# A stored order of steps in place of a list scheduler, in a fused attention and feed-forward kernel

## The chip, the cores and the metric

The kernel runs on one core of one Trainium2 chip. The metric is the device time of one execution in microseconds; the median of several runs is given, and one further execution was recorded by the hardware profiler. Engines are named as the profile names them: PE is TensorE (PEld its weight loads), DVE is VectorE, ACT is ScalarE, POOL is GpSimd, and SP is SyncE, which here only issues DMA transfers.

## What is computed

Attention with a soft cap on the scores, over 4 batches, 12 heads, 448 positions and 64 columns a head, then a feed-forward block with a sigmoid gate on the 1792 x 768 result:

```python
def _attn_ref(q, k, v, cap) -> np.ndarray:
    scale = 1.0 / np.sqrt(q.shape[-1])
    scores = scale * np.matmul(q, k.transpose(0, 1, 3, 2))
    scores = cap * np.tanh(scores / cap)
    scores = scores - np.max(scores, axis=-1, keepdims=True)
    attn = np.exp(scores)
    attn = attn / (np.sum(attn, axis=-1, keepdims=True) + 1e-09)
    return np.matmul(attn, v).astype(np.float32)

def _moe_ref(x, w_in, w_out) -> np.ndarray:   # x is attention's output, 1792 x 768
    h = x @ w_in                              # 768 x 2048
    g = h * (1.0 / (1.0 + np.exp(-1.702 * h)))
    return (g @ w_out).astype(np.float32)     # 2048 x 768
```

All inputs and the output are f32. The soft cap is 30, so the exponentials need no row maximum.

## The kernel before, in words

**Units.** The attention runs in 24 units, one for a batch and a pair of heads. The first 8 units multiply in f32; the other 16 split each operand into an f16 part and an f16 remainder and multiply the parts. For one unit, `scores` writes products of K and Q to PSUM (`s`, two banks in turn), ACT takes the tanh (`t`) and the exponential, and the result lies as `p`, in a ring of five tiles. In f16 units the exponential is split: a copy `p<-t` makes the high part (a step that ACT or DVE may do), and DVE's subtraction `p<-t,p` the low one. `row_sums`, `part_sums` and a few others multiply `p` by ones to get the row sums (`sm`), and `col_tiled` multiplies `p` by V (`pa`). The sums take a way through DRAM: `f<-sm`, then the transfers `sd`, `rsum`, a reciprocal `rr`, `rd`, and `rb`, the inverse sums spread over the partitions. DVE multiplies `pa` by `rb`, and the result is split again (`x` or `xa`, high and low).

**Feed-forward.** The weights arrive as raw words and are decoded on DVE and ACT (`g` and `wo` for the first pieces of `w_in`; `wi_h` and `wi_l` are the parts). For batches 0 and 1, `h_unit` multiplies x by `w_in` into `m`, the gate follows on ACT and DVE (`f`, `g`), and `o_unit` multiplies `g` by `w_out`, in `m` as well. Batches 2 and 3 share sums of blocks, seven products in place of eight, in `m` and `z`; they fill the time from about 400 us on.

**Shapes on the PE array.** Full products (`m`, `z`, most of the f16 `s`) use the whole 128 x 128 array. `pa` uses tiles of 128 rows by 64 columns, `sm` tiles of 128 by 32, and the f32 `s` tiles of 64 by 128 or 64 by 64. A step carries the shape's name in its field `turn`.

**What sets the order.** Nothing of this is issued as it is written. The class `Plan` records every step as an `Op`: the engines that may do it, with a cost on each (`ways`), its dependences, and the rings of buffers from which it takes tiles. `scaled` (L194) records a step with two ways, ACT (`on_act`) and DVE (`on_dve`), unless it is told one. `mm`, `act`, `dve` and `dma` record steps for PE, ACT, DVE and SP. When all is recorded, `schedule` (L331) decides: 30 times a list scheduler (`forward`, L243) takes the step that can start first by the costs, with the engine among its ways and the ring slot that is free, and `backward` (L295) works out by when each step is due, which gives the priorities of the next pass. The best pass is kept. Then `refine` (L412) tries to move short runs of PE steps of one tile shape next to another run of that shape, up to 20 us away, and keeps a move if `timed` (L367) gives a shorter total. In these costs a change of tile shape on PE is put down at a fixed price:

```python
PE_TURN = 0.093
...
                if e == "PE":
                    us += PE_TURN * (o.turn != turn)
                    turn = o.turn
```

`emit` (L451) then issues the steps in that order, under a manual schedule, and each engine runs its own in a row. `keep_busy` can put small matmuls into gaps early on, and adds none in this kernel. A flag computed at the end guards a general path, which does not run with these inputs. In the profile nearly all instructions have the line of the helper that issues them: L218 for matmuls, L183 for DVE, L175 and L199 for ACT, L202 to L206 for `scaled` steps on DVE, L224 for transfers.

Of the kernel before, what the change touches and what calls it, by code (L numbers as in the profile page):

```python
# [35 lines left out]
PASSES = 30  # L36
# [21 lines left out]
DVE_SHY = (1.0,)  # L58
STAY = (0.0,)
ROUNDS, RUN, REACH = 4, 6, 20.0  # L60
# [48 lines left out]
class Plan:  # L109
# [118 lines left out]
    def start_over(self):  # L228
        bufs = {b for o in self.ops for b in o.bufs}
        for b in bufs:  # L230
            b.left, b.freed = 0, 0.0
            if b.ring:
                b.slot = None
        for o in self.ops:
            o.left, o.ready = len(o.deps), 0.0
            o.eng = next(iter(o.ways)) if len(o.ways) == 1 else None
            for b in o.bufs:
                b.left += 1
        for r in self.rings:
            r["free"] = [(0.0, i) for i in range(len(r["tiles"]))]  # L240
            r["queue"] = list(r["turns"])

    def forward(self, shy, stay=0.0):  # L243

        self.start_over()
        free = {"PE": 0.0, "ACT": ACT_FROM, "DVE": ACT_FROM, "SP": 0.0}
        cand = {e: [o for o in self.ops if e in o.ways and not o.left] for e in free}
        turn, pipe = None, 0.0
        order = []
        while len(order) < len(self.ops):  # L250
            best = None
            for e, c in cand.items():
                for o in c:
                    t = max(o.ready + (shy if e == "DVE" and len(o.ways) > 1 else 0.0), free[e])
                    for b in o.bufs:
                        if b.slot is None:
                            r = b.ring
                            t = max(t, r["free"][0][0]) if r["free"] and (r["any"] or r["queue"][0] is b) else math.inf
                    k = (t, o.prio + (stay if e == "PE" and o.turn != turn else 0.0), o.ways[e][0])
                    if best is None or k < best[0]:  # L260
                        best = (k, e, o)
            assert best is not None and best[0][0] < math.inf, "no step can go on"
            (t, _, us), e, o = best
            for w in o.ways:
                cand[w].remove(o)
            o.eng, o.emit = e, o.ways[e][1]
            for b in o.bufs:
                if b.slot is None:
                    b.ring["queue"].remove(b)
                    b.slot = b.ring["free"].pop(0)[1]  # L270
            if e == "PE":
                us += PE_TURN * (o.turn != turn)
                turn = o.turn
            o.start, o.end = t, t + us
            free[e] = t + us
            done = t + us + LAG[e]
            if e == "SP":
                pipe = max(pipe, t + us) + o.mb / DMA_BW
                done = pipe + LAG[e]
            order.append(o)  # L280
            for u in o.users:
                u.left -= 1
                u.ready = max(u.ready, t + us if u.eng == e == "PE" else done + HANDOFF)
                if not u.left:
                    for w in u.ways:
                        cand[w].append(u)
            for b in o.bufs:
                b.left -= 1
                b.freed = max(b.freed, done + HANDOFF)
                if not b.left and b.ring:  # L290
                    b.ring["free"].append((b.freed, b.slot))
                    b.ring["free"].sort()
        return order

    def backward(self, order):  # L295

        after = {o: [(u, 0.0 if u.eng == o.eng == "PE" else LAG[o.eng] + HANDOFF) for u in o.users] for o in order}
        turns = {}
        for o in order:
            for b in o.bufs:  # L300
                if b.ring:
                    x = turns.setdefault((id(b.ring), b.slot), [])
                    if not x or x[-1][0] is not b:
                        x.append((b, []))
                    x[-1][1].append(o)
        for x in turns.values():
            for (_, was), (_, then) in zip(x, x[1:]):
                for o in was:
                    after[o].append((then[0], LAG[o.eng] + HANDOFF))
        before = {o: [] for o in order}  # L310
        for o, xs in after.items():
            for u, lag in xs:
                before[u].append((o, lag))
        left = {o: len(xs) for o, xs in after.items()}
        end = max(o.end for o in order)
        due = {o: end for o in order}
        free = dict.fromkeys(("PE", "ACT", "DVE", "SP"), end)
        cand = [o for o in order if not left[o]]
        start = {}
        while cand:  # L320
            o = max(cand, key=lambda o: (min(due[o], free[o.eng]), o.end))
            cand.remove(o)
            free[o.eng] = start[o] = min(due[o], free[o.eng]) - (o.end - o.start)
            for q, lag in before[o]:
                due[q] = min(due[q], start[o] - lag)
                left[q] -= 1
                if not left[q]:
                    cand.append(q)
        return start

    def schedule(self):  # L331

        best = None
# [33 lines left out]
    def timed(self, pre, seqs, limit=math.inf):  # L367
# [5 lines left out]
        turn, pipe, left = None, 0.0, n  # L373
        while left:
            moved = False
            for e, s in seqs.items():
                k = at[e]
                while k < len(s):
                    i = s[k]
                    t = free[e]  # L380
                    for p, near in pre[i]:
                        if start[p] is None:
                            t = None
                            break
                        x = end[p] if near else done[p] + HANDOFF
                        if x > t:
                            t = x
                    if t is None:
                        break
                    o = self.order[i]  # L390
                    us = o.ways[e][0]
# [4 lines left out]
                    free[e] = t + us  # L396
                    if e == "SP":
                        pipe = max(pipe, t + us) + o.mb / DMA_BW
                        done[i] = pipe + LAG[e]
                    else:  # L400
                        done[i] = t + us + LAG[e]
                    if end[i] > limit:
                        return None
                    k += 1
                    left -= 1
                    moved = True
                at[e] = k
            if not moved:
                return None
        return start, end, max(end)  # L410

    def refine(self, rounds):  # L412

        pre = self.edges()
        seqs = {e: [i for i, o in enumerate(self.order) if o.eng == e] for e in ("PE", "ACT", "DVE", "SP")}
        start, end, best = self.timed(pre, seqs)
        for _ in range(rounds):
            gained = False
            k = 1
            while k < len(seqs["PE"]):  # L420
                s = seqs["PE"]
                turn = lambda j: self.order[s[j]].turn
                if turn(k) == turn(k - 1):
                    k += 1
                    continue
# [18 lines left out]
            if not gained:  # L444
                break
# [1110 lines left out]
```

## Time and profile before

| what | value |
|---|---|
| time, median of 3 runs | 603.84 us (603.43 to 603.88) |
| the profiled execution | 603.16 us, of which 600.9 us is the span from first to last instruction |
| PE busy | 589.3 us (98%) |
| DVE busy | 540.5 us (90%) |
| ACT busy | 414.2 us (69%) |
| TensorE's granted clock, mean | 0.998 |
| chain that ended last | PE 86%, DVE 5%, DMA 4% |

The 2.3 us between the span and the time lie outside of the recorded instructions. Busy shares are an average over the span: attention ends a little after 400 us, and the engines beside PE have more room behind that. Line numbers in rows are those of the kernel before.

### The profile page before, as it was taken

What the parts mean: (1) busy time and instruction counts of PE and PEld (TensorE: products, weight loads), DVE (VectorE), ACT (ScalarE), POOL (GpSimd) and SP (SyncE); (2) the same over time, 40 slices, a digit from 0 to 9 for tenths busy, and PEclk for the clock granted to TensorE, in tenths of its full rate; (3) what the DMA queues carried; (4) which work ended last, traced back from release to release, by engine and by line L of the source; (5) the groups of instructions that cost most, each with busy time, mean ns of one, the idle gap of its engine ahead of it and who ended that gap; (6) DMA issues with size and microseconds to landing.
All of it is one profiled execution on the core that took longest, in us unless ns stands there. A gap on an engine that the chain in (4) does not pass through costs nothing.

```text
span 600.9 us, 9852 instructions
## 1 busy us (share of the span) xinstructions
PE 589.3 (98%) x3666; PEld 281.5 (47%) x3666; DVE 540.5 (90%) x898; ACT 414.2 (69%) x610; POOL 0.2 (0%) x4
## 2 busy tenths in 40 slices
PE   7999999999999999999999999999999999999995
PEld 3332344444544444445554445455555555555552
DVE  4999999999999999999999989878999999968912
ACT  5998896999987987999879779834555554211100
POOL 0000000000000000000000000000000000000000
PEclk9999999999999999999999999999999999999999
DMA  8988864226567443513343453022222210001001
GB/s 297 383 234 246 296 220 149 81 53 208 154 193 231 157 130 87 178 46 109 109 122 130 127 174 120 30 83 58 71 76 65 53 54 1 31 15 47 32 15 50
DMA packets 45556, 73.87 MB, mean 123 GB/s; under 512 B 14952, under 2 KB 31168, under 8 KB 45504
## 3 DMA queue, kind: packets, MB, share of 16 engines
q1 hardware_dynamic: 45504, 73.20, 38.4%
q8 instruction: 30, 0.49, 0.3%
q14 instruction: 22, 0.18, 0.1%
HBM read 61.22 MB, written 11.95 MB: 122 GB/s over the span
## 4 chain that ended last, share of the span: by engine, by line
PE 86%; DVE 5%; DMA 4%; ACT 2%; issue 1%; SPq 1%; DVEq 0%; ACTq 0%
PE m L218 43%; PE z L218 22%; PE s L218 9%; PE pa L218 9%; PE sm L218 3%; DMA wo<-in_moe_w_in_dram 1%; DMA rd<-rr 1%; ACT t L175 1%; SPq L224 1%; DVE ta L183 1%; DMA stg<-in_kx_dram 1%; DVE p L183 1%; ACT p L175 1%; DMA wo<-in_q_dram 1%; DVE f L183 0%
## 5 line engine op out<-in xcount | busy, mean ns | idle before, releaser
L218 PE MATMUL m<-g,wo 128*128 128x448 f16 x624 | 127.4, 353 | 0.0
L218 PEld LDWEIGHTS <-wo 128*128 128x128 f16 x864 | 81.8, 98 | 82.0 <-issue 9.0
L175 ACT ACTIVATE t<-s,tsc 128x896 f32<-128x896 f32 x96 | 86.8, 918 | 17.4 <-PE s L218 13.7
L218 PEld LDWEIGHTS <-wi_h 128*128 128x128 f16 x528 | 49.4, 98 | 56.2 <-issue 12.2
L218 PE MATMUL m<-x,wi_h 128*128 128x448 f16 x234 | 63.6, 353 | 0.0
L175 ACT ACTIVATE t<-t,lnb,capt 128x896 f32<-128x896 f32 (+1 forms) x58 | 59.4, 1030 | 0.4
L183 DVE TENSOR_TENSOR p<-t,p 128x896 f16<-128x896 f32 (+1 forms) x58 | 55.2, 954 | 4.1 <-ACT p L199 3.7
L218 PE MATMUL m<-xa,wi_h 128*128 128x448 f16 x198 | 53.7, 353 | 0.0
L218 PE MATMUL s<-qh,kk 128*128 128x448 f16 (+3 forms) x160 | 48.1, 403 | 0.0
L199 ACT ACTIVATE p<-t 128x896 f16<-128x896 f32 (+1 forms) x54 | 45.1, 838 | 0.3
L183 DVE SCALAR_TENSOR_TENSOR wo<-wo 128x1024 int32<-128x1024 int32 (+2 forms) x42 | 43.8, 1064 | 0.0
L218 PE MATMUL m<-x,wi_l 128*128 128x448 f16 x117 | 41.2, 352 | 0.0
L218 PEld LDWEIGHTS <-stg 128*128 128x128 f16 x288 | 28.2, 98 | 26.3
L218 PE MATMUL s<-ql,kk 128*128 128x448 f16 (+1 forms) x128 | 39.6, 352 | 0.0
L218 PEld LDWEIGHTS <-wi_l 128*128 128x128 f16 x264 | 25.8, 98 | 24.1
L199 ACT ACTIVATE xa<-x 128x1024 f16<-128x1024 f32 x9 | 9.5, 1057 | 38.3 <-PE z L218 27.3
L218 PE MATMUL pa<-p,vh 128*64 128x448 f16 x256 | 35.6, 356 | 0.4 <-DVE rb L183 0.4
L218 PE MATMUL m<-xa,wi_l 128*128 128x448 f16 x99 | 34.9, 352 | 0.0
L218 PEld LDWEIGHTS <-kk 128*128 128x128 f16 (+1 forms) x256 | 20.8, 100 | 23.4 <-issue 6.8
L218 PE MATMUL sm<-p,ones 128*32 128x224 f16 (+2 forms) x544 | 30.8, 313 | 0.5 <-ACT p L175 0.5
L218 PEld LDWEIGHTS <-xa 128*128 128x128 f16 x216 | 21.1, 98 | 19.6
L175 ACT ACTIVATE p<-t,capt 128x896 f32<-128x896 f32 (+1 forms) x32 | 29.6, 970 | 0.0
(282 smaller groups left out, 1078.4 us busy)
## 6 DMA issues: line engine op xcount, KB each, us to landing
wo<-in_moe_w_in_dram SPq DMA_DIRECT2D x18, 512.0 KB
stg<-in_kx_dram SPq DMA_DIRECT2D x16, 448.0 KB
stg<-in_qx_dram SPq DMA_DIRECT2D x16, 448.0 KB
stg<-in_moe_w_out_dram SPq DMA_DIRECT2D x16, 384.0 KB
wo<-in_moe_w_out_dram SPq DMA_DIRECT2D x16, 384.0 KB
sum<-xa SPq DMA_DIRECT2D x32, 192.0 KB
stg<-sum SPq DMA_DIRECT2D x32, 192.0 KB
rb<-rd SPq DMA_DIRECT2D x44, 112.0 KB
```

Of the source, the lines that this page charges most:

```text
L175: self.nc.scalar.activation(real(out), real(in_), func, scale=real(scale), **b)
L183: getattr(self.nc.vector, name)(out=real(out), **{k: real(x) for k, x in ins.items()}, **kw, **a)
L199: self.nc.scalar.activation(real(out), real(in_), AF.Copy, scale=1.0 if f is None else f, **b)
L218: self.nc.tensor.matmul(real(o), real(w), real(x), start=a, stop=z)
L224: self.nc.sync.dma_start(real(o), real(i))
```

## The change

The list scheduler (`start_over`, `forward`, `backward`, `refine` and their constants) is taken out. In its place stands `ORDER`, a packed table with two parts: for each position, the number of a recorded step, its top bit saying which of the step's ways is taken; then, for each turn of each ring, the slot that it gets. `schedule` reads it, sets engine and slot of each step, lets `timed` work out start times along these rows, and sorts by them. The recording of the steps, their costs, their dependences and `emit` are as before. In the core of the diff one line of the table stands for all:

```diff
-PASSES = 30
...
-DVE_SHY = (1.0,)
-STAY = (0.0,)
-ROUNDS, RUN, REACH = 4, 6, 20.0
+
+ORDER = (
...
+    "ki+XIFzmw1TBXsd@Z^xe5gQD*3AaNRo_dCZ!(SO558+Jz2#bGrF#mV>AJ%H1p#"
+)
...
     def schedule(self):
 
-        best = None
-        for i in range(PASSES):
-            stay = STAY[i % len(STAY)] if i else 0.0
-            order = self.forward(DVE_SHY[0], stay)
-            total = max(o.end for o in order)
-            if best is None or total < best[0]:
-                best = (total, stay, {o: o.prio for o in order})
-            for o, t in self.backward(order).items():
-                o.prio = t
-        for o, p in best[2].items():
-            o.prio = p
-        self.order = self.forward(DVE_SHY[0], best[1])
-        self.refine(ROUNDS)
+        n = len(self.ops)
+        raw = zlib.decompress(base64.b85decode(ORDER))
+        slots = iter(raw[2 * n:])
+        for r in self.rings:
+            for b in r["turns"]:
+                b.slot = next(slots)
+        self.order = []
+        for x in struct.unpack(f"<{n}H", raw[:2 * n]):
+            o = self.ops[x & 0x7FFF]
+            o.eng = list(o.ways)[x >> 15]
+            o.emit = o.ways[o.eng][1]
+            self.order.append(o)
+        seqs = {e: [i for i, o in enumerate(self.order) if o.eng == e] for e in LAG}
+        start, end, self.total = self.timed(self.edges(), seqs)
+        for i, o in enumerate(self.order):
+            o.start, o.end = start[i], end[i]
+        self.order = [self.order[i] for i in sorted(range(n), key=lambda i: (start[i], i))]
```

The instructions themselves are the same, but for the 15 more `scaled` steps that go to DVE than before. What the table moves is shown at four places. A row is one instruction, or several alike that follow one another: its line, its operation, what it writes and reads, and the shape of what it writes; the number behind a name is that of the tensor.

**First, SP at the head of the program, before.** `wo` is a ring of staging tiles here, into which `k`, `q` and `v` of the f32 units are loaded; `g` takes the first four pieces of `w_in`.

```order
L524 DMA capt<-in_cap_dram 128x1
L224 DMA wo<-in_k_dram 128x448
L224 DMA wo<-in_q_dram 128x448
L224 DMA wo<-in_v_dram 128x512
L224 DMA wo<-in_k_dram 128x448
L224 DMA wo<-in_q_dram 128x448
L224 DMA g<-in_moe_w_in_dram 128x1024 x4
```

And SP at the head after:

```order
L408 DMA capt<-in_cap_dram 128x1
L263 DMA wo<-in_k_dram 128x448
L263 DMA wo<-in_q_dram 128x448
L263 DMA g<-in_moe_w_in_dram 128x1024 x2
L263 DMA wo<-in_v_dram 128x512
L263 DMA wo<-in_k_dram 128x448
L263 DMA wo<-in_q_dram 128x448
L263 DMA g<-in_moe_w_in_dram 128x1024 x2
```

Two of the four pieces of `w_in` have moved ahead of the first `v` and the second `k` and `q`.

**Second, PE in the f32 units, some 60 rows from its start, before.** Here `s`, `pa` and `sm` read K, V and ones.

```order
L218 MATMUL s_160<-wo 128x448 x2
L218 MATMUL pa_156<-p_136,wo 64x448 x2
L218 MATMUL sm_155<-p_137,ones_2_75 32x224 x4
L218 MATMUL sm_155<-p_138,ones_2_75 32x224 x4
L218 MATMUL s_161<-wo 128x448 x2
L218 MATMUL s_160<-wo 128x448 x2
L218 MATMUL sm_155<-p_134,ones_2_75 32x224 x4
L218 MATMUL sm_155<-p_135,ones_0_73 32x224 x2
L218 MATMUL sm_155<-p_135,ones_1_74 32x224 x2
L218 MATMUL pa_156<-p_137,wo 64x448 x2
L218 MATMUL pa_156<-p_138,wo 64x448 x2
```

PE at the same distance from its start, after:

```order
L257 MATMUL pa_156<-p_138,wo 64x448 x2
L257 MATMUL pa_156<-p_134,wo 64x448 x2
L257 MATMUL pa_156<-p_135,wo 64x448 x2
L257 MATMUL pa_156<-p_136,wo 64x448 x2
L257 MATMUL s_161<-wo 128x448 x2
L257 MATMUL s_160<-wo 128x448 x2
L257 MATMUL sm_155<-p_137,ones_2_75 32x224 x4
L257 MATMUL sm_155<-p_138,ones_2_75 32x224 x4
L257 MATMUL sm_155<-p_134,ones_2_75 32x224 x4
L257 MATMUL sm_155<-p_135,ones_0_73 32x224 x2
L257 MATMUL sm_155<-p_135,ones_1_74 32x224 x2
```

The eleven rows have six stretches of one shape before and three after.

**Third, PE in the f16 units, where the row sums of one `p` tile end, before.** Each f16 matmul has a weight load of its own ahead of it.

```order
L218 LDWEIGHTS ones_2_78
L218 MATMUL sm_155<-p_135,ones_2_78 32x224
L218 LDWEIGHTS wo
L218 MATMUL m_92<-g,wo 128x448
L218 LDWEIGHTS wo
```

And where the row sums of the last `p` tile of a unit end, after:

```order
L257 LDWEIGHTS ones_1_77
L257 MATMUL sm_155<-p_138,ones_1_77 32x224
L257 LDWEIGHTS vh_147
L257 MATMUL pa_156<-p_135,vh_147 64x448
L257 LDWEIGHTS vh_147
```

Before, the sums stop after `p_135`, twelve matmuls of `m` follow, and the sums of `p_136` come after them; after, the sums of all tiles stand together and `pa` follows them at once.

**Fourth, DVE in an f16 unit, before.** `ta` collects sums of `t`.

```order
L183 TENSOR_TENSOR p_138<-t_131,p_138 128x896
L183 SCALAR_TENSOR_TENSOR ql_130<-stg_123,qh_128 128x896
L183 TENSOR_TENSOR ta_133<-ta_133,t_132 64x448
L183 TENSOR_TENSOR p_134<-t_132,p_134 128x448
L183 TENSOR_TENSOR ta_133<-ta_133,t_132 64x448
```

The same tiles after:

```order
L222 TENSOR_TENSOR ta_133<-ta_133,t_132 64x448
L222 TENSOR_TENSOR p_138<-t_131,p_138 128x896
L243 CAST p_134<-t_132 128x448
L222 TENSOR_TENSOR ta_133<-ta_133,t_132 64x448
L222 TENSOR_TENSOR p_134<-t_132,p_134 128x448
```

The cast of `p_134` to its high part, on ACT before, has moved into DVE's row, two instructions ahead of the subtraction that reads it.

## Rows read from the trace of the kernel before

**Rows 1.** The page: busy time by engine, and the chain by engine.

```profile
PE 589.3 (98%) x3666; PEld 281.5 (47%) x3666; DVE 540.5 (90%) x898; ACT 414.2 (69%) x610; POOL 0.2 (0%) x4
...
PE 86%; DVE 5%; DMA 4%; ACT 2%; issue 1%; SPq 1%; DVEq 0%; ACTq 0%
```

**Rows 2.** PE's waits after its start: releaser, us in total, times, longest.

```profile
PE s L218 <- ACT t L175: 1.1, 2, 0.8
PE sm L218 <- ACT p L175: 0.5, 1, 0.5
PE pa L218 <- DVE rb L183: 0.4, 2, 0.2
```

**Rows 3.** Windows (from:to, length, busy by engine, PE's clock, DMA share, GB/s).

```profile
0.00:20.00 20.00, 16.37 (x100) 6.65 (x100) 10.84 (x37) 13.98 (x18) 0.20 (x4) 1.00 0.89 328
20.00:350.00 330.00, 328.22 (x2166) 150.72 (x2165) 323.56 (x514) 291.20 (x418) 0.00 (x0) 1.00 0.52 163
350.00:601.00 251.00, 244.72 (x1404) 124.17 (x1402) 206.08 (x350) 109.02 (x176) 0.00 (x0) 1.00 0.18 54
```

**Rows 4.** Pieces of the chain: start, duration, what (matmuls in a row).

```profile
16.81 1.71 PE s L218 x8
...
68.38 0.90 PE pa L218 x4
69.28 0.95 PE s L218 x4
...
75.16 0.89 PE sm L218 x16
...
77.86 1.65 PE pa L218 x8
...
110.51 1.65 PE sm L218 x32
...
126.83 1.26 PE pa L218 x12
...
148.52 0.30 PE sm L218 x8
...
162.81 0.50 PE sm L218 x16
...
170.29 1.14 PE m L218 x6
171.43 2.39 PE pa L218 x24
173.82 1.24 PE m L218 x6
```

**Rows 5.** DVE's groups by form: shapes, count, busy us, mean ns, idle before.

```profile
L206 DVE TENSOR_SCALAR wo<-wo 128x1024 f32<-128x1024 f32 x5 | 3.5, 691 | 0.0
L206 DVE TENSOR_SCALAR kk<-stg 128x896 f16<-128x896 f32 x5 | 3.1, 620 | 0.0
...
L204 DVE CAST p<-t 128x896 f16<-128x896 f32 x4 | 2.5, 618 | 0.0
...
L206 DVE TENSOR_SCALAR g<-f 128x448 f16<-128x448 f32 x5 | 1.9, 378 | 0.0
...
L202 DVE TENSOR_SCALAR f<-sm 128x224 f32<-128x224 f32 x2 | 0.8, 387 | 0.0
L206 DVE TENSOR_SCALAR wo<-stg 128x384 f16<-128x384 f32 x2 | 0.7, 356 | 0.0
```

**Rows 6.** Timeline of DVE's first decoding step: start, us, [idle before it].

```profile
9.23 0.43 DVE L183 TENSOR_SCALAR g<-g 128x512 int32<-128x512 int32 x1 [5.00 <-DMA g<-in_moe_w_in_dram]
```

**Rows 7.** Timeline at a `pa` that waits for DVE, from 292.0 us.

```profile
292.01 0.62 DVE L183 TENSOR_TENSOR rb<-pa,rb 128x448 f32<-128x448 f32 x1
...
292.54 1.08 DVE L183 TENSOR_TENSOR p<-t,p 128x896 f16<-128x896 f32 x1
...
292.68 0.57 PE L218 MATMUL pa<-p,vh 128*64 128x448 f16 x4 [0.16 <-DVE rb L183]
```

More of the change, by code (lines that the diff above doesn't have):

```diff
@@ L1 @@
+import base64
 import math
+import struct
+import zlib
 from contextlib import ExitStack
@@ L225, in dma @@
         self.op({"SP": (DMA_ISSUE * len(pairs), emit)}, [p[0] for p in pairs], [p[1] for p in pairs], mb=mb)
[L228 to L238, printed above, removed]
-        for r in self.rings:
-            r["free"] = [(0.0, i) for i in range(len(r["tiles"]))]
-            r["queue"] = list(r["turns"])
@@ L243, in forward @@
[L243 to L250, printed above, removed]
-            best = None
[L252 to L329, printed above, removed]
@@ L365, in edges, with timed @@
         return [list(dict(sorted(p)).items()) for p in pre]
-    def timed(self, pre, seqs, limit=math.inf):
+    def timed(self, pre, seqs):
         n = len(self.order)
@@ L372, in timed @@
         free = {"PE": 0.0, "ACT": ACT_FROM, "DVE": ACT_FROM, "SP": 0.0}
-        turn, pipe, left = None, 0.0, n
-        while left:
+        turn, pipe = None, 0.0
+        while any(at[e] < len(s) for e, s in seqs.items()):
             moved = False
             for e, s in seqs.items():
[L377 to L389, printed above, removed]
+                while at[e] < len(s) and all(start[p] is not None for p, _ in pre[s[at[e]]]):
+                    i = s[at[e]]
                     o = self.order[i]
+                    t = max([free[e]] + [end[p] if near else done[p] + HANDOFF for p, near in pre[i]])
                     us = o.ways[e][0]
@@ L395, in timed @@
                     start[i], end[i] = t, t + us
-                    free[e] = t + us
+                    free[e] = done[i] = t + us
                     if e == "SP":
[L398 to L405, printed above, removed]
+                        done[i] = pipe = max(pipe, t + us) + o.mb / DMA_BW
@@ L406, in timed @@
+                    done[i] += LAG[e]
+                    at[e] += 1
                     moved = True
-                at[e] = k
-            if not moved:
-                return None
+            assert moved, "no step can go on"
         return start, end, max(end)
[L412 to L425, printed above, removed]
-                m = k
-                while m < len(s) and turn(m) == turn(k):
-                    m += 1
-                run, tries = s[k:m], []
-                if len(run) <= RUN:
-                    for step in (-1, 1):
-                        j = k - 1 if step < 0 else m
-                        while 0 <= j < len(s) and abs(start[s[j]] - start[s[k]]) < REACH:
-                            if turn(j) == turn(k):
-                                tries.append(s[:j + 1] + run + s[j + 1:k] + s[m:] if step < 0 else s[:k] + s[m:j] + run + s[j:])
-                                break
-                            j += step
-                for new in tries:
-                    got = self.timed(pre, {**seqs, "PE": new}, best + 2.0)
-                    if got and got[2] < best - 0.005:
-                        (start, end, best), seqs["PE"], gained = got, new, True
-                        break
-                k = m
-            if not gained:
-                break
-        for i, o in enumerate(self.order):
-            o.start, o.end = start[i], end[i]
-        self.order = [self.order[i] for i in sorted(range(len(start)), key=lambda i: (start[i], i))]
-        self.total = best
```

39 lines of the change are left out of this document (37 added, 2 removed).

## Prediction, made before the changed kernel was run

> **What bounds the kernel now.** I read the page first: TensorE (PE) is busy for 589.3 of 600.9 us, VectorE (DVE) for 540.5, ScalarE (ACT) for 414.2, and 86% of the chain that ended last is PE [rows 1]. PE's busy time alone proves little, since a matmul's end is modelled and matmuls overlap, so I looked next at what PE waits for. After the first score matmuls there are three entries, 1.1, 0.5 and 0.4 us [rows 2]. PE runs one matmul after another, and its granted clock is 1.00 (the 2.4 GHz level) in every stretch [rows 3], so the clock is not in question. The time can fall in two ways: PE's stream gets cheaper, or its few waits go. The same windows show who comes second. From 20 to 350 us DVE is busy for 323.56 of 330.00 us [rows 3], so it has 6.4 us of room there. After 350 us it has 45 us, and before 20 us it mostly waits for its first weights: 5.00 us ahead of its first decoding step at 9.23 [rows 6].
>
> The chain of waits then shows a price inside PE's stream that no idle time shows. Six full-array products `m` that follow one another take 1.14 us, and the same six right after a row of `pa` (128x64 tiles) take 1.24 [rows 4]. A change of tile shape costs 0.10 us.
>
> **Part 1: fewer changes of tile shape.** The matmuls are the same 3401 in both kernels, and only their order differs. I counted along PE's order the places where the tile shape (rows x columns of the array) differs from that of the matmul before: 188 before, 104 after. The two places of PE in the section on the change show the pattern: `s`, `pa` and `sm` alternate before, and stand together now. By shape and type, runs before and after, with the price from the chain [rows 4]:
> - full array: 68 to 32. Price 1.24 - 1.14 = 0.10. 36 x 0.10 = 3.6 us.
> - 128x64 with f16 (`pa`): 33 to 17. Twelve cost 1.26 and 24 cost 2.39, so 12 cost 1.13 and the change 0.13. 16 x 0.13 = 2.1 us.
> - 128x32 with f16 (`sm`): 26 to 11. Eight cost 0.30 and 16 cost 0.50, so the change costs 0.10. 15 x 0.10 = 1.5 us.
> - 128x64 with f32: 21 to 11. Four cost 0.90 and eight 1.65, so the change costs 0.15. 10 x 0.15 = 1.5 us.
> - 128x32 with f32: 16 to 13. Sixteen cost 0.89 and 32 cost 1.65, so 0.13. 3 x 0.13 = 0.4 us.
> - the two f32 shapes of `s`: 25 to 23. Four cost 0.95 and eight 1.71, so 0.19. 2 x 0.19 = 0.4 us.
>
> The sum is 9.5 us; with the price of each kind averaged over all its runs in the trace it is 9.8, and I take **9.6 us**. It lies wholly on the path, since PE has no room to hide it. By place in the order, about 66 of the lost changes (7.8 us) lie before 350 us, the stretch in which DVE is nearly full, and 16 (1.8 us) between 350 and 400 us.
>
> **Part 2: fifteen scaling steps go from ACT to DVE.** DVE has 892 instructions for 877, ACT 594 for 609. By form: seven more casts of `p` at 128x896 (0.618 us), two at 128x448 (no row; the nearest, a scaling of that size, has 0.378), four more `f<-sm` (0.387), four more 128x448 scalings to f16 (0.378) and four more at 384 columns (0.356), 9.6 us in all [rows 5]. Against them stand two fewer 128x896 scalings (0.620), two of 1024 columns (0.691), one of 512 (between these and 0.378, taken as 0.42) and one `pu` copy (like the casts, 0.62): 3.7 us. The net is +5.9 us of durations. DVE's next instruction starts before the last one ends: `rb` runs from 292.01 to 292.63 and the next begins at 292.54 [rows 7]. With 0.08 of overlap for each of 15 steps, DVE's own time grows by **4.7 us**. ACT loses about 8 us, which is worth nothing by itself: it is busy for 291 of 330 us in the same stretch [rows 3].
>
> The Trainium skill, "VectorE: DVE Perf Modes", section "The DRAIN you can't avoid", says that the next DVE operation does not start until the pipe of the one before is empty, except where it isn't held. Taken as it stands for each added step it would make the 4.7 us the full 5.9, and the forecast below about 1 us longer; the rows at 292.54 go against it at that place.
>
> **Part 3: what DVE gives back.** A matmul that needs a DVE result comes at the later of two times: PE's own work ahead of it, and DVE's work up to and with that result plus DVE's idle time. For each such matmul I added PE's work ahead (rates and prices of [rows 4], from the first matmul at 5.15 us) and DVE's work (each step by its row of the same form, less the overlap), along the order of either kernel. The difference is the cushion. The smallest ones, before and after:
> - near 120 us: 127.1 - 120.6 = 6.5 before; 115.3 - 111.5 = 3.8 after
> - near 200 us: 202.4 - 195.8 = 6.6; 204.3 - 199.9 = 4.4
> - near 287 us: 287.6 - 280.3 = 7.3; 287.2 - 282.7 = 4.5
> - near 303 us: 303.4 - 295.7 = 7.7; 301.8 - 297.0 = 4.7
> - near 350 us: 13.3 before; 6.6 after. Later ones are 14.9 or more in both.
>
> The third of them can be laid against the trace: that `pa` starts at 292.68, 0.16 us after PE fell idle, right behind `rb`, which ends at 292.63 [rows 7]. So PE stood 5.1 us behind its own work there, and DVE 12.3 us. With the new order and DVE still 12.3 us behind, the awaited `rb` ends at 282.7 + 12.3 = 295.0, and PE, whose own work says 287.2, is 7.8 us behind: **2.7 us** more than before. The fourth gives 2.4 in the same way. Had DVE's steps kept their places in front of PE's needs, the cushion would have shrunk by the whole 7.8 + 4.7 us; it shrinks by 2.2 to 2.9 up to 305 us, so the new order brings what PE awaits earlier in DVE's row.
>
> At the head the first pieces of `w_in` (`g`) are issued after two loads in place of five, so DVE's 5.00 us of waiting [rows 6] shrinks; two pieces still come behind four others, and the head's decode steps now stand next to one another and wait for each other. I take 0.3 us, nearer to nothing than to the 2 us by which the first piece may come earlier. The given-back time is 2.7 - 0.3 = **2.4 us**, with bounds of 0 (all hidden) and 4.7 (every moved step paid).
>
> Past 440 us the smallest loop from PE through DVE back to PE tightens as well, by my count from about 7 us of slack to about 1; I price that at nothing, with 1.5 us as its upper bound. SP issues the same transfers in another order. Behind the head, the row sums' way through DRAM (`sd`, `rsum`, `rd`, `rb`) has 8.5 to 11.8 us of DVE work between the reciprocal and the product that needs `rb`, where it had 7 to 8.3, so it is priced at nothing; if `rb` came late, PE would stand at its `pa` as at 292.68 [rows 7]. The tail behind the last product is the same steps in both, at nothing too.
>
> **Sum.** The profiled run took 603.16 us. 603.16 - 9.6 + 2.4 = 595.96 us. That run lies 0.68 us under the median of the runs (603.84), so the forecast for the median is **596.6 us**, with 594.2 (nothing given back) to 598.9 (4.7 given back) as its own range.
>
> **Rivals.**
> - **A, nothing is given back.** DVE starts so much earlier at the head, or has so much slack in its idle 6.4 us, that PE keeps all 9.6: 594.2 us. For it: PE before waits for DVE only 0.4 us in all [rows 2]. Against it: the cushions at 290 to 305 us have no slack in the trace [rows 7].
> - **B, VectorE is the true bound from 20 to 350 us.** Then every result that PE awaits comes later by the 4.7 us added, less 0.3 at the head, what PE saves before 350 us is lost in waiting, and only the 1.8 us after it remain: 603.84 + 4.4 - 1.8 = 606.4 us, slower. For it: 323.56 of 330.00 us busy [rows 3]. Against it: the count above, by which DVE's order has moved ahead by most of the difference. It decides where the cushion shrinks by some 10 us rather than 2.7.
> - **C, the rows of one shape hold buffers.** `sm` and `pa` of a unit now stand together, so they need all five `p` buffers filled, and a split of `p` (1.08 us [rows 7]) may be exposed in each of the 16 f16 units: 17.3 - 9.6 gives 611.5 us; it breaks even at 0.6 us for each unit. Against it: `pa` already runs 24 in a row before [rows 4], with all five filled.
> - **D, gain and losses cancel:** half of B or C, near 603.8 us.
>
> **How the numbers follow.** Forecast 0.75, A 0.12, B 0.05, C 0.03, D 0.05. About 0.2% (1.2 us) is what a measurement of this kernel can tell from no change. The forecast and A lie beyond it on the fast side: faster 0.87, same 0.05, slower 0.08. The range goes from 593.5 (A with a little more from the head) to 601.5 (the forecast with the 4.7 us, the 1.5 us past 440 and the price of the overlap), which leaves out B, C, D and a little of the forecast's tail.
>
> **What the profile after would show.** Part 1 is right if `m x6` still costs 1.14 or 1.24, the long rows of one shape stand in the chain, and PE's busy time falls to near 580. Part 2: DVE near 545, ACT near 406. Part 3: PE's waits for DVE rise from 0.4 to 2 to 3 us, mostly on `pa`, `sm` and `m` between 80 and 310 us. If PE waits 5 us or more for DVE there, B has begun; if it waits for `p` from ACT or DVE at every unit's `sm`, C. The forecast is wrong if a change of shape costs less when `sm` and `pa` stand next to each other, or if DVE waits for ACT, DMA or PSUM where it did not before.

## The result

The kernel with the stored order took 595.57 us (median of 4 runs, 595.3 to 596.48), the kernel before 603.86 us in the same session (603.43 to 604.53). The ratio is 0.9864, with a 95% interval of 0.9847 to 0.9881: faster by 1.2 to 1.5%. The forecast for the median was 596.6. The execution that the profiler recorded took 595.59 us; the prediction's sum for it was 595.96.

The page of the changed kernel, busy time by engine and the chain that ended last by engine, to lay beside [rows 1]:

```profile
PE 580.4 (98%) x3666; PEld 288.4 (49%) x3666; DVE 545.3 (92%) x913; ACT 406.5 (69%) x595; POOL 0.2 (0%) x4
...
PE 72%; DVE 16%; DMA 6%; issue 3%; SPq 1%; ACT 1%; DVEq 0%
```

PE is busy for 8.9 us less, DVE for 4.8 more and ACT for 7.7 less, near the 580, 545 and 406 that the prediction named. (The rule of the Trainium skill, "VectorE: DVE Perf Modes", section "The DRAIN you can't avoid", taken for every added step without the exception that the page makes for steps that aren't held, would have made DVE's added time the full 5.9 us. The 4.8 sides with the overlap seen in [rows 7].) PE's share of the chain has fallen from 86% to 72%, so more of what released PE was somewhere else. What PE waits for after its start, to lay beside [rows 2] (engine, line, releaser: us in all, times, longest):

```profile
PE s L257 <- ACT t L214: 2.1, 3, 1.2
...
PE m L257 <- DVE f L222: 0.6, 2, 0.5
PE m L257 <- DVE x L222: 0.5, 1, 0.5
PE pa L257 <- DVE rb L222: 0.2, 1, 0.2
```

PE's waits for DVE are 1.3 us where they were 0.4, and its largest entry is `s` waiting for ACT. Two things are to be told apart, then: how cheap PE's stream became, and how much later it runs. For the second I use one measure throughout. **Lateness** is the start of a matmul less PE's own work ahead of it (every matmul and every change of shape at the prices of [rows 4], from 5.15 us on). It grows by what PE loses in waits, or to a lower clock, whatever a row calls them. In us, at marks of PE's own work:

| kernel | own work in all | at 20 | 40 | 60 | 98 | 200 | 287 | 350 | 575 |
|---|---|---|---|---|---|---|---|---|---|
| before | 589.4 | 2.0 | 3.1 | 4.2 | 4.2 | 4.3 | 4.8 | 5.1 | 5.3 |
| changed | 579.6 | 2.3 | 3.7 | 5.7 | 6.5 | 6.4 | 6.9 | 7.2 | 7.4 |

The profiled executions differ by 7.57 us. Own work accounts for 9.8 of gain, lateness for 2.1 of loss, and the rest is under 0.2. The prediction had 9.6 and 2.4. But the loss does not arise where it was forecast. After the mark at 98 us the kernel before loses 1.1 us and the changed one 0.9. The whole difference stands by then: 0.6 us at the mark of 40, 1.5 at 60 and 2.3 at 98. Own work is counted by prices and not measured, so a wrong price would show as lateness. Some 60 of the lost changes, about 7 us of them, lie behind 98 us, and lateness rises alike there in both kernels, which speaks for the prices.

### The profile page after: what moved, and what is told of

The parts are those of the page before. It is cut to its first block, busy times and chain, and to the rows that moved or that the text cites. A ratio compares the mean times of both kernels' runs of the same rounds, so it can differ in the third digit from the quotient of the medians.

```text
span 593.4 us, 9800 instructions
## 1 busy us (share of the span) xinstructions
PE 580.4 (98%) x3666; PEld 288.4 (49%) x3666; DVE 545.3 (92%) x913; ACT 406.5 (69%) x595; POOL 0.2 (0%) x4
## 4 chain that ended last, share of the span: by engine, by line
PE 72%; DVE 16%; DMA 6%; issue 3%; SPq 1%; ACT 1%; DVEq 0%
PE m L257 36%; PE z L257 22%; PE s L257 6%; PE pa L257 6%; DVE ta L222 2%; DVE p L222 2%; PE sm L257 2%; DVE wo L222 2%; DMA wo<-in_moe_w_in_dram 1%; DVE rb L222 1%; DMA wo<-in_v_dram 1%; DVE f L222 1%; DVE kk L222 1%; DMA rsum<-sd 1%; DVE pu L222 1%
## 5 line engine op out<-in xcount | busy, mean ns | idle before, releaser
L257 PEld LDWEIGHTS <-wo 128*128 128x128 f16 x864 | 83.2, 98 | 80.9 <-issue 4.9
L214 ACT ACTIVATE t<-s,tsc 128x896 f32<-128x896 f32 (+1 forms) x96 | 86.3, 908 | 19.8 <-PE s L257 8.8
L257 PEld LDWEIGHTS <-wi_h 128*128 128x128 f16 x528 | 50.6, 98 | 52.7 <-issue 6.8
L238 ACT ACTIVATE p<-t 128x896 f16<-128x896 f32 (+1 forms) x47 | 38.8, 833 | 4.9 <-PE pa L257 4.5
L257 PEld LDWEIGHTS <-kk 128*128 128x128 f16 (+1 forms) x256 | 22.2, 101 | 21.1 <-issue 2.0
L257 PE MATMUL s<-wo 64*128 64x448 f32 (+1 forms) x96 | 24.6, 624 | 2.5 <-DMA wo<-in_q_dram 1.3
```

What stands on the lines that cost most here:

```text
L214: self.nc.scalar.activation(real(out), real(in_), func, scale=real(scale), **b)
L238: self.nc.scalar.activation(real(out), real(in_), AF.Copy, scale=1.0 if f is None else f, **b)
L257: self.nc.tensor.matmul(real(o), real(w), real(x), start=a, stop=z)
```

## The experiments

Each kernel is the changed one with the edit named, unless another is said. Sessions differ (the kernel before took 603.86 to 606.40 us), so times are compared by their ratio to the kernel before of the same session, or by lateness in the profiles. The changed kernel's own ratio was 0.9864, and 0.9832 when run again, so less than some 2 us between two sessions says little by itself.

### Do the changes of shape cost what the chain says?

**split_late** puts 54 changes of shape back between 100 and 400 us, by moving products `m` in between `pa`, on PE alone. It serves to time PE's stream, not to compute the result:

```diff
 MATMUL pa_156<-p_137,vl_148 64x448
+MATMUL m_91<-x,wi_h 128x448
+MATMUL m_91<-x,wi_h 128x448
+MATMUL m_91<-x,wi_l 128x448
 MATMUL pa_156<-p_138,vh_147 64x448
```

> The changed kernel with the same engines and the same order on DVE, ACT and SP; on PE alone, steps of m are moved in between the pa steps of the f16 units, so that 54 more changes of tile shape stand between 100 and 400 us (27 into 128x64, 27 back to the full array). Theory of the prediction (a change costs 0.10 to 0.13 us wherever it stands and lies on the path): 54 x 0.115 = 6.2 us, so 601.8 us. Rival (the gain came from better waits, and changes are hidden or overlap): within 2 us of the changed kernel, 595.6 to 597.6 us.

It took 602.17 us, 0.9959 (0.9945 to 0.9973) of the kernel before: 5.7 us above the changed kernel by the two ratios, 6.6 by the medians. Its page:

```profile
PE 587.4 (98%) x3666; PEld 283.4 (47%) x3666; DVE 546.4 (91%) x913; ACT 407.0 (68%) x595; POOL 0.2 (0%) x4
```

PE is busy for 7.0 us more with the same matmuls. Own work by the prices of [rows 4] grows by 6.1 us, and lateness ends at 7.8 where it was 7.4, so little else moved. A change of shape costs 0.11 to 0.12 us there (5.7 to 6.6 us for 54), and all of it is paid.

**split_head** puts 14 changes back ahead of 70 us, again on PE alone:

```diff
 MATMUL pa_156<-p_135,wo 64x448 x2
+MATMUL sm_155<-p_134,ones_2_75 32x224 x4
+MATMUL sm_155<-p_135,ones_2_75 32x224 x4
 MATMUL pa_156<-p_136,wo 64x448 x2
 MATMUL s_161<-wo 128x448 x2
 MATMUL s_160<-wo 128x448 x2
-MATMUL sm_155<-p_134,ones_2_75 32x224 x4
-MATMUL sm_155<-p_135,ones_2_75 32x224 x4
```

> The changed kernel with 14 more changes of tile shape on PE ahead of 70 us, in the f32 units, by moves of single PE steps past at most four others; nothing else is moved. Theory of the prediction (every change lies wholly on the path): 14 x 0.15 = 2.1 us, so 597.7 us. Rival (up to about 70 us the loads and ACT set the pace, and what PE saves there is given back there): at most 0.6 us more than the changed kernel, 595.6 to 596.2 us.

596.87 us, 0.9871 (0.9846 to 0.9896), which can't be told from the changed kernel's 0.9864. Own work grows by 2.1 us, and lateness ends 1.3 lower (6.1). By that, a good half of what PE's own stream costs in the head would be hidden in waits that PE has there anyway. But the interval reaches up to 1.9 us above the changed kernel, and two executions of the changed kernel itself differ by 1.7 us in lateness at the mark of 60 (after_again, below), so the share isn't settled.

### Is PE's order alone enough?

**pe_order_alone** keeps the engines and the DVE, ACT and SP orders of the kernel before, and gives PE an order with 121 changes of shape for 187 (the prediction's 188 takes in the first matmul). One place, against the kernel before:

```diff
 MATMUL pa_156<-p_134,wo 64x448 x2
-MATMUL s_160<-qh_128,kk_126 128x448 x2
 MATMUL pa_156<-p_135,wo 64x448 x2
 MATMUL pa_156<-p_136,wo 64x448 x2
 MATMUL pa_156<-p_137,wo 64x448 x2
+MATMUL s_160<-qh_128,kk_126 128x448 x2
+MATMUL s_161<-qh_128,kk_126 128x448 x2
```

> The kernel before with the same engines and the same order on DVE, ACT and SP; only PE's order is changed, so that its tile shape changes 121 times in place of 187. PE's own work falls by 7.2 us by the prices of the rows of before. Theory of the prediction (what PE gets from DVE bounds it: the cushion near 283 us falls from 7.3 to 2.8 us, as DVE's steps keep their places): PE gives back about 4.3 us of it, so about 601.0 us. Rival 1 (PE's stream decides alone): 596.7 us. Rival 2 (VectorE is the bound and all is given back): 603.8 us.

606.04 us, 1.0017 (1.0001 to 1.0033): no gain at all. Own work falls by 7.8 us, and lateness ends at 14.6 for 5.3. Some 3.6 us of that loss stand by the mark at 98: ahead of it PE waits 3.5 us for `p`, `t` and `f` from ACT, for 1.6 in the kernel before. PE's waits from 100 to 594 us:

```profile
PE pa L257 <- DVE rb L222: 2.1, 4, 1.1
PE m L257 <- DVE f L222: 1.2, 4, 0.4
PE s L257 <- ACT t L214: 0.4, 1, 0.4
PE sm L257 <- DVE p L222: 0.3, 1, 0.3
```

The kernel before has only the `pa` entry there, at 0.4 us. Behind 100 us this is near rival B's mechanism, brought about by leaving DVE's order as it was: a shorter stream on PE arrives earlier at results that do not. Its row for 100 to 350 us (length, busy time of PE, PEld, DVE, ACT and POOL, clock, DMA share, GB/s), and below it the same of the kernel before and of the changed one:

```profile
100.00:350.00 250.00, 246.19 (x1692) 125.27 (x1692) 244.26 (x415) 217.28 (x320) 0.00 (x0) 1.00 0.46 138
```

```profile
100.00:350.00 250.00, 249.63 (x1697) 121.80 (x1696) 245.52 (x418) 218.48 (x321) 0.00 (x0) 1.00 0.45 137
```

```profile
100.00:350.00 250.00, 249.56 (x1727) 128.40 (x1727) 246.80 (x421) 220.15 (x318) 0.00 (x0) 1.00 0.46 137
```

PE loses 3.4 us of busy time, and DVE 1.3 of its own: DVE waits for PE and ACT in turn. My sum for this kernel, 601.0, held DVE's idle time fixed and missed by some 4 us (1.0017 of 603.84 is 604.9). In the changed kernel PE is as busy as before there (within 0.1 us), DVE and ACT are busier, and the same stretch holds 30 more matmuls. With this one order, then, PE alone gains nothing; in the changed kernel the gain comes with the order of all engines together.

### What are the steps that went from ACT to DVE worth?

**back10** and **back_late** give 54 late steps back to the engine that they had before (33 to ACT, 21 to DVE) and fit DVE's and ACT's orders to that; PE's and SP's orders stay. One place of back_late:

```diff
 DVE  SCALAR_TENSOR_TENSOR f_139<-f_139,m_92 128x448
-DVE  TENSOR_SCALAR wo<-stg_124 128x384
 DVE  SCALAR_TENSOR_TENSOR xa<-rb_142,xa 128x448
 DVE  SCALAR_TENSOR_TENSOR wo<-stg_124,wo 128x384
-DVE  TENSOR_SCALAR wo<-stg_121 128x384
```

> The changed kernel with its order on PE and SP, but the 54 steps behind 75 us whose engine the table changed go back to the engine they had before (33 of them back to ACT, 21 to DVE); DVE's work falls by 4.3 us, ACT's grows by 6.3, and the order of DVE and ACT is fitted anew to the same PE order. Theory of the prediction (the 4.7 us more on DVE is what PE gives back): 593.4 to 594.0 us. Rival (the room on DVE is needed by ACT as much, the smallest cushions become 3.2 to 4.2 us near 145 to 251 us for 3.8 to 4.5, and PE waits as long or longer): 595.6 to 597.0 us.

back10 took 605.11 us, 0.9996 (0.9977 to 1.0015). It says little on its question: the fitting changed DVE's order in the first 20 us too, and lateness was already past 9 by 75 us. So back_late keeps the changed kernel's order ahead of 75 us.

> As back10, but with everything ahead of 75 us in the changed kernel's order on every engine: the 54 steps behind 75 us whose engine the table changed go back to the engine they had before (33 to ACT, 21 to DVE; DVE's work falls by 4.3 us, ACT's grows by 6.3), each put at the best place in its new row, and few others move. PE's and SP's order is that of the changed kernel. Theory of the prediction (what PE gives back comes from DVE's added work): 593.4 to 594.0 us. Rival (ACT is bound as closely as DVE, and the two feed each other): 596 us or more; by the smallest cushion (2.8 us near 204 us for 4.4) about 596.6 to 597.2 us.

598.28 us, 0.9889 (0.9872 to 0.9905), 1.5 us slower than the changed kernel by the ratios, though DVE is busy for 3.5 us less (541.8). head_dve and act_twice below, which have the changed kernel's late order, took 596.3 and 596.09 in the same session. Lateness grows by 2.8 us between the marks at 200 and 287 (the changed kernel: 0.5) and ends at 9.9 for 7.4. The longest of DVE's own waits from 100 to 350 us in back_late, and the same wait in the changed kernel:

```profile
DVE p L222 <- ACT p L238: 1.9, 5, 0.8
```

```profile
DVE p L222 <- ACT p L238: 0.2, 1, 0.2
```

DVE waits for `p` from ACT, five times. So the late moves, both ways and with the order fitted to them, bring 1.5 to 2.5 us: they make DVE busier, and it waits less. What the moves bring without that order, no run shows (back_late also has DVE wait 0.9 us for a load, which the changed kernel has not).

### What is lost ahead of 60 us?

PE's first products `m` need `x`, and `x` comes through a chain: the sums `f` go to DRAM (`sd`) and come back (`rsum`), DVE takes the reciprocal (`rr`), `rd` and `rb` go the same way once more, and DVE multiplies. DVE's waits from 20 to 75 us, all of them, in the kernel before and in the changed one:

```profile
DVE wo L183 <- DMA wo<-in_moe_w_in_dram: 1.9, 2, 1.3
```

```profile
DVE rr L222 <- DMA rsum<-sd: 1.8, 1, 1.8
DVE f L241 <- PE sm L257: 0.8, 1, 0.8
DVE rb L222 <- DMA rb<-rd: 0.7, 1, 0.7
DVE wo L222 <- DMA wo<-in_moe_w_in_dram: 0.2, 1, 0.2
```

Where the time to spare went, in the timeline: SP's issue of the third `rsum` and DVE's reciprocal of it (start, us, what), before and after:

```profile
36.37 2.23 SPq L224 DMA_DIRECT2D rsum<-sd  x1
...
45.63 0.19 DVE L183 RECIPROCAL rr<-rsum 112x8 f32<-112x8 f32 x1
```

```profile
37.75 1.18 SPq L263 DMA_DIRECT2D wo<-in_moe_w_in_dram  x2
39.23 0.33 SPq L263 DMA_DIRECT2D rsum<-sd  x1
...
46.18 0.20 DVE L222 RECIPROCAL rr<-rsum 112x8 f32<-112x8 f32 x1 [1.78 <-DMA rsum<-sd]
```

Before, DVE reached its four reciprocals 6.7, 8.4, 9.3 and 6.1 us after SP issued their `rsum`. Now it would reach them after 5.2, 4.1, 5.2 (6.95 less the wait) and 5.8. The third transfer carries 3.5 KB, is queued behind two pieces of 512 KB, and its row in the chain of waits is longer than that:

```profile
39.23 6.93 DMA rsum<-sd
```

Four kernels try this stretch. **head_dve** moves two DVE steps later, so that other work fills the waits:

```diff
+SCALAR_TENSOR_TENSOR wo<-wo 128x1024 x2
-SCALAR_TENSOR_TENSOR wo<-wo 128x1024
 TENSOR_SCALAR f_140<-sm_155 128x224
-SCALAR_TENSOR_TENSOR wo<-wo 128x1024
 ...
+TENSOR_SCALAR wo<-wo 128x1024
+SCALAR_TENSOR_TENSOR wo<-wo 128x1024
 RECIPROCAL rr_149<-rsum 112x8
-TENSOR_SCALAR wo<-wo 128x1024
-SCALAR_TENSOR_TENSOR wo<-wo 128x1024
```

> The changed kernel with two DVE steps moved later in the head: one f<-sm (it waits 0.79 us for PE at 23.2 us) past one decoding step, and one reciprocal rr (it waits 1.78 us for the transfer rsum at 46.2 us) past two decoding steps. Theory (DVE's idle time in the head is what PE has to give back by 105 us): DVE gains up to 2.5 us there, and the time falls by 1 to 2 us, to 593.6 to 594.6 us. Rival (DVE would have waited for its weights as well, or ACT holds PE up to 60 us): within 0.4 us of the changed kernel, 595.2 to 596.0 us.

596.3 us, 0.986 (0.9843 to 0.9877): no gain. DVE's waits from 20 to 75 us have other names:

```profile
DVE wo L222 <- DMA wo<-in_moe_w_in_dram: 2.6, 2, 1.3
DVE wi_l L222 <- ACT wi_h L238: 1.0, 1, 1.0
...
DVE rr L222 <- DMA rsum<-sd: 0.2, 1, 0.2
```

The wait for `rsum` is gone, 1.8 to 0.2 us, and the one for weights is back. So that one transfer is not all that holds DVE here; it may be what the queue has to bring as a whole, which no run tested.

**dve_twice** does two of DVE's decode steps (`wi_l`, at 50 and 53 us) twice, **act_twice** two of ACT's exponentials at 40 to 50 us (steps 183 and 200 in the same line):

```diff
+            if x & 0x7FFF in (197, 50):
+                o.emit = lambda f=o.emit: (f(), f())
```

> The changed kernel with two of DVE's decoding steps (wi_l, 1.14 us each from start to start) in the stretch from 50 to 56 us done twice: 2.3 us more work on DVE, nothing else changed. Theory (from the head on, PE waits for what DVE delivers, and every us on DVE there is one on PE): 597.5 to 597.9 us. Rival (PE or ACT sets the pace there and DVE has room): at most 596.2 us.

> The changed kernel with two of ACT's exponentials (p from t, 0.96 us each from start to start) in the stretch from 40 to 50 us done twice: 1.9 us more work on ACT, nothing else changed. Theory (up to 60 us ACT sets the pace of the f32 units): 597.0 to 597.5 us if it is still felt behind the head, by which PE would have to be later at 98 us than DVE makes it. Rival (DVE's results at 90 to 105 us set PE's time, whatever ACT does ahead of 60 us): at most 596.2 us.

dve_twice took 599.37 us, 0.9905 (0.9888 to 0.9921), act_twice 596.09, 0.9853 (0.9836 to 0.9869). DVE's 2.3 added us come back as 2.5 by the ratios (3.8 in lateness at the mark of 60, of which part is a lower clock, below). ACT's 1.9 us cost nothing that can be measured. So between 50 and 60 us PE follows DVE, and ACT has room from 40 us on, though PE's list of waits names ACT's `t` first: ahead of the later two of those three waits ACT itself waits for `wo` from DVE (1.4 us at its `wi_h`). The first and longest lies ahead of the steps that dve_twice and act_twice repeat:

```profile
37.72 1.02 PE L257 MATMUL s<-wo 64*128 64x448 f32 x4 [1.19 <-ACT t L214]
```

ACT has no gap of 0.1 us from 30 us to the end of that `t` at 37.57, so PE follows ACT there, and no run made ACT faster at this place.

**after_again** is the changed kernel, run again:

> The changed kernel once more, as the reference for the next two on the same chip: 0.9864 of the kernel before, as in the first result, by every theory.

596.05 us, 0.9832 (0.9817 to 0.9847). In this execution `rsum` is later, and so is everything behind it:

```profile
DVE rr L222 <- DMA rsum<-sd: 3.4, 1, 3.4
```

The wait is 1.6 us longer than in the first execution, and lateness at the mark of 60 is 7.4 for 5.7. So the same program differs from itself by 1.7 us, here with a transfer that takes longer; what those 1.7 us are made of stands in the last section.

**dve_less** makes DVE's work from 58 to 78 us cheaper by 6.1 us by count (5.5 by its page, 539.8 busy); it leaves out two reciprocals and two minima:

```diff
-        plan.dve("tensor_reduce", new_rmin(), dict(in_=s4), n=S, op=ALU.min, axis=AX.X)
+        plan.op({"DVE": (..., lambda: nc.vector.memset(real(rm), 2.0**20))}, [rm], [s4])
-        plan.dve("reciprocal", r, dict(in_=s4), kind="recip")
+        plan.op({"DVE": (..., lambda: nc.vector.tensor_scalar_mul(real(r), real(s4), 2.65e-13))}, [r], [s4])
```

> The changed kernel with less work on DVE between 58 and 78 us, all orders kept: the reciprocals of the row sums of the two units that are normalised without the way through DRAM are left out (each a scaling by one constant in their place, 0.38 us for 2.9), and the two minima over their row sums that only feed the flag (0.6 us each, small fills in their place). DVE's work falls by about 6.1 us there. Theory (behind the head PE is late by what DVE delivers, and ACT and the loads hold PE only up to 72 us): the matmul that waits for DVE at 98 us of PE's own work, late by 6.5 us in the changed kernel, becomes late by 5.8, its lateness at 72 us; the end is early by that and by the 0.9 us that come later, 0.7 to 1.6 us under the changed kernel. Rival 1 (DVE alone sets the time): 5 us or more under it. Rival 2 (DVE is not waited for there): within 0.4 us of it.

596.11 us, 0.984 (0.9819 to 0.9861): no gain. Lateness grows by 0.1 between the marks at 60 and 98, where the changed kernel has 0.8 and 0.4 in its two executions. That execution was 7.0 late by the mark of 60, and lateness once there does not fall. What DVE does between the marks at 60 and 98 adds at most 0.8 us in the changed kernel.

### Can a table with more room do better?

**slack3** and **slack4** are tables searched further, so that by the planner's count DVE could run 3 or 4 us late without cost. They have 105 and 108 changes of shape (the changed kernel 104, counted alike). The head of DVE's order in slack4:

```diff
 SCALAR_TENSOR_TENSOR wi_l<-wo,wi_h 128x2x512
-SCALAR_TENSOR_TENSOR wo<-wo 128x1024
-RECIPROCAL rr_150<-rsum 112x8
-SCALAR_TENSOR_TENSOR wi_l<-g,wi_h 128x2x512
 SCALAR_TENSOR_TENSOR x<-rb_143,x 128x448
-SCALAR_TENSOR_TENSOR wi_l<-wo,wi_h 128x2x512
 TENSOR_SCALAR wo<-wo 128x1024
+TENSOR_SCALAR stg_123<-stg_123 128x384
 SCALAR_TENSOR_TENSOR wo<-wo 128x1024
+RECIPROCAL rr_150<-rsum 112x8
```

> The changed kernel's table, searched further behind 47 us on all four engines with the same steps on the same engines, so that 3 us of delay on DVE at 43 us cost PE nothing by the planner's costs. PE has 105 changes of tile shape as the changed kernel and the same work of its own; the smallest cushions are 5.5 near 99 us, 5.2 near 132, 5.8 near 299, for 3.9, 3.8 and 4.5. Theory (behind the head PE is late by DVE's idle time less the cushion, and the head's idle time is what it is): PE is 1.3 to 1.6 us less late, so 1.3 to 1.6 us under the changed kernel, a ratio to the kernel before of 0.9838 to 0.9843. Rival (PE's lateness comes from the head's loads and ACT whatever the order behind it): within 0.4 us of the changed kernel, 0.9857 to 0.9871.

> As slack3, searched against 4 us of delay: 108 changes of tile shape (0.4 us more work on PE), smallest cushions 6.4 near 98 us, 5.9 near 135, 5.4 near 188, 5.5 near 260. Theory: PE is 1.5 us less late for 0.4 us more work, so about 1.1 us under the changed kernel, a ratio of 0.9846. Rival: 0.4 us above the changed kernel or more, 0.9871 or more.

Neither theory held: slack3 took 599.25 us, 0.9878 (0.9858 to 0.9898), slack4 598.58, 0.9861 (0.9839 to 0.9884), beside 596.05 and 0.9832 (0.9817 to 0.9847) of after_again in the same session. slack3 is slower; slack4 is slower by the medians, but the intervals overlap. slack3's lateness is 8.9 at the mark of 98 and 13.0 at the end; DVE's largest wait in the head is at the second half of the same way through DRAM:

```profile
DVE rb L222 <- DMA rb<-rd: 3.7, 2, 3.0
```

slack4 does repair the head (lateness 3.8 at 60 and 5.3 at 98, for 5.7 and 6.5), and then loses 3.8 us behind it, to 9.1. The room that the planner counted was not there on the chip. None of these kernels beats the changed one.

## Why the prediction was right, and where not

**Part 1 held.** It is 9.8 us of own work for the forecast's 9.6, and the price of a change between `m` and `pa` stood the test of split_late. (The prediction's list by kind has 82 of the 84 lost changes; the two that it lacks, one each of the two kinds of 128x64, are the 0.3 us between its 9.5 and 9.8.) The six products `m` that the prediction put up as its sign cost the same as in [rows 4], 1.13 among themselves and 1.24 behind another shape (rows of the chain of waits; long rows of one shape stand there too):

```profile
110.00 1.65 PE sm L257 x32
...
154.59 2.39 PE pa L257 x24
166.74 1.13 PE m L257 x6
...
331.01 1.24 PE m L257 x6
```

"It lies wholly on the path" is not borne out ahead of about 60 us, where by split_head a part may be hidden. Seven of the 84 lost changes lie in the first 50 us of own work, so the sum hardly noticed.

**Part 2 was right in DVE's own time, and wrong on what ACT's relief is worth.** DVE's 4.7 us are 4.8. That ACT's relief "is worth nothing by itself" is not borne out: where back_late gives ACT its late work back, 1.5 to 2.5 us are lost (order and moves together). ACT is not full there, but DVE waits for single results of it.

**Part 3 held as a rule and in size; its place was wrong.** At the third place of its list the awaited `rb` was put at 295.0 us, and PE 7.8 behind its own work. The timeline:

```profile
293.77 0.62 DVE L222 TENSOR_TENSOR rb<-pa,rb 128x448 f32<-128x448 f32 x1
...
294.44 0.57 PE L257 MATMUL pa<-p,vh 128*64 128x448 f16 x4
```

`rb` ends at 294.39, so DVE stands 11.7 us behind its own work (294.39 - 282.7) where 12.3 was assumed, and PE 7.2 (294.44 - 287.2). At the fourth place PE is 7.2 behind too (309.0 for 301.8). But the same rule had bound already before the first place on that list, at 89 us:

```profile
88.13 0.61 DVE L222 SCALAR_TENSOR_TENSOR f<-f,m 128x448 f32<-128x448 f32 x1
...
88.79 0.54 PE L257 MATMUL m<-x,wi_h 128*128 128x448 f16 x2 [0.45 <-DVE f L222]
```

By the count of the prediction DVE's own work up to that `f` is 78.1 us, so DVE stands 10.6 behind (88.74 - 78.1), and PE, with 82.3 of own work, 6.5. Lateness is the largest that any place has forced so far, not their sum, so a later place that forces 7.2 costs 0.7 more. The forecast that PE would wait for DVE 2 to 3 us between 80 and 310 fell with that: those waits are 1.3 us in the whole run. The loss is made in the head. The prediction's own sign of being wrong, that DVE waits for DMA where it did not before, appeared there: 1.8 us for `rsum` and 0.7 for `rb`.

The terms that were mis-sized stand there. The row sums' way through DRAM was "priced at nothing". It was counted for its second half alone, from the reciprocal to the product. The first half, from `rsum`'s issue to the reciprocal, went from between 6.1 and 9.3 us down to between 4.1 and 5.8, against a transfer of 6.93. The head's gain was taken as 0.3 us. In fact DVE has done 2.07 us more by 20 us (12.91 for 10.84 of [rows 3]; its first step starts at 7.66 for 9.23), and most of it is lost again by 60 us, with 3.4 us of idle time from 20 to 60 where it had 1.9. The two errors cancel: DVE's idle time up to the third place falls by 0.6 us, near the 0.3 that stood in the sum. To that extent the sum was lucky, and the second profiled execution of the same program (after_again), with its `rsum` later still, gives back 1.7 us more by the mark of 60.

**The rivals.** A (nothing given back, 594.2) fell: 2.1 us were given back. B's mechanism is real, as pe_order_alone shows, but the change moves DVE's order along with PE's, and DVE kept up. C did not appear: PE's waits behind 100 us hold no entry for `p`. D would have needed half of B or of C, and the time is 8 us away from it.

**What stays open.** How the loss ahead of the mark of 60 is shared out between the weights' loads, the row sums and ACT is not settled: head_dve took one wait of DVE away and got the other, and no run eased ACT at 37 us. Nor is it known why slack4 loses 3.8 us behind 98 us, where by its count it had room.

## What to carry to other kernels

On an engine that never idles, read the price of a change of shape from the chain of waits, where the same row of matmuls stands with and without it, and count the changes; that term held within some ten per cent. Reordering one engine alone gave the whole gain back here, so read a reordering by lateness at several marks (start less own work), which tells where a loss is made when the names of waits only change. Give a small transfer that is issued behind big ones their time too, in both directions of a way through DRAM: here 3.5 KB took 6.93 us behind two pieces of 512 KB, though no run moved it ahead of them.

## What the chip showed that I had not expected

A wait of PE can cost more than its length on the spot. In after_again PE waits 2.23 us for `x`, and the granted clock falls (windows of 2 us; the columns as above), from 1.00, the 2.4 GHz level, to 0.50, the 1.2 GHz level, and back:

```profile
48.00:50.00 2.00, 0.40 (x3) 0.11 (x2) 1.97 (x4) 1.76 (x3) 0.00 (x0) 1.00 1.33 203
50.00:52.00 2.00, 1.37 (x4) 0.55 (x4) 2.00 (x5) 1.10 (x2) 0.00 (x0) 0.65 0.49 134
52.00:54.00 2.00, 2.00 (x6) 0.84 (x6) 2.00 (x4) 0.21 (x1) 0.00 (x0) 0.50 0.56 164
54.00:56.00 2.00, 2.00 (x12) 0.67 (x10) 2.00 (x3) 1.82 (x2) 0.00 (x0) 0.99 0.88 234
```

The matmuls behind that wait, in this execution and then in the changed kernel's first one, whose wait there is 0.45 us:

```profile
50.63 0.53 PE L257 MATMUL m<-x,wi_h 128*128 128x448 f16 x1 [2.23 <-DVE x L222]
...
52.58 2.47 PE L257 MATMUL s<-wo 64*128 64x448 f32 x8
54.98 1.72 PE L257 MATMUL sm<-p,ones 128*64 128x448 f32 x8
...
65.48 3.18 PE L257 MATMUL pa<-p,wo 128*64 128x448 f32 x16
```

```profile
49.35 0.35 PE L257 MATMUL m<-x,wi_h 128*128 128x448 f16 x1 [0.45 <-DVE x L222]
...
50.39 1.77 PE L257 MATMUL s<-wo 64*128 64x448 f32 x8
52.09 1.72 PE L257 MATMUL sm<-p,ones 128*64 128x448 f32 x8
...
58.98 1.02 PE L257 MATMUL s<-qh,kk 64*128 64x448 f32 x4 [0.35 <-ACT t L214]
60.51 1.02 PE L257 MATMUL s<-qh,kk 64*128 64x448 f32 x4 [0.51 <-ACT t L214]
...
63.85 3.18 PE L257 MATMUL pa<-p,wo 128*64 128x448 f32 x16
```

From that `m` to `sm` it is 4.35 us (54.98 - 50.63) for 2.74 (52.09 - 49.35), so the lower clock takes 1.6 us on top of the 2.2 waited. Most of that comes back at once: `sm` is 2.89 us later than in the first execution, but the `pa` below it only 1.63 (65.48 for 63.85), since PE's two waits for `t` there are gone. That 1.63 is the difference in lateness between the two: 1.28 from the later `x` and 1.6 from the clock, less 1.25 made up. A stretch of 20 us with a mean clock of 0.91 stands in dve_twice as well (60 to 80 us, behind waits of 1.62 and 0.52 us for `t`), and in dve_less (40 to 60 us, behind one of 1.88 us for `x`), beside 1.00 in the first execution of the changed kernel, where PE's wait of 1.19 us at 37.72 left the clock at 1.00.
